# A spectral filter and an MLP in one kernel: the first batch's last inverse pair by way of DRAM, with four first-stage units of the second batch in front of it

## The chip, the cores and the metric

The kernel runs on one core of one Trainium2 chip. A core has TensorE (PE, matrix products), VectorE (DVE), ScalarE (ACT), GpSimd (POOL), and SyncE (SP), which here only issues DMAs; DMAs are also issued from ACT's and POOL's queues. The metric is the device time of one execution in microseconds (us).

## The reference

```
x: (8, 3008, 256)   filt: (1505, 256) complex   w_in: (256, 2048)   w_out: (2048, 256)   all float32
X = rfft(x, axis=1);  y = irfft(X * filt, n=3008, axis=1)          # for each of 8 batches
h = y.reshape(24064, 256) @ w_in
out = (h * clip(h + 3, 0, 6) / 6) @ w_out
```

## The kernel before

**The transform.** 3008 = 47 x 64, so the real FFT is done in two stages for 24 frequencies k of the stage of 47. Stage 1 (`a_unit`: 16 small matmuls over 4 of the 32 columns, eight units for a batch) writes an intermediate z to DRAM (`z_store`, four DMAs a unit). Stage 2 (`b_unit`) reads it back, `f_unit` multiplies by the filter on DVE, `y_unit` forms the complex products, and `bi_unit` is the first stage of the inverse; its result g goes to DRAM (`g_store`, two DMAs of 256 KB). The units of stage 2 go by two k each, 12 units (0 to 11) for a batch; `bi_unit` takes two units at once, and is called here *pair 0, 2, ... 10* by its first unit. The second stage of the inverse (`n_first`, `n_unit`, `n_five`) reads g back transposed into the tile `t4`, k on partitions, multiplies it with a table and leaves the tokens of y in the SBUF ring `xn`.

**The MLP.** The 24064 tokens are worked off in 47 blocks of 512, each in 8 steps of 256 hidden columns. Block 0 is done plainly: in step p `plain_up(p)` (L789) makes the hidden values, ACT the relu (L726), DVE the gate g (`hswish`, L731), and `plain_down(p-1)` (L800) multiplies the previous step's g by w_out. From block 1 on a Strassen-like scheme is used (L681, L757).

**The weights** come as 64-bit words (`load_bits`, 16 parts of 512 KB) and are turned into float32: ACT takes the absolute high word (`w_abs`, L321), DVE does seven operations (`w_conv`, `w_conv_2`, L330 to L353). `convert(n)` does n parts in one go, `convert_half` one half of a part; the list `(3, 3, 3, 4, 4, 3, 2, 2)` says how many halves follow the gates of each step of block 0.

**Order.** Nothing is rearranged: each engine's instructions stand in the order in which the program text issues them. Batch 0 is transformed ahead of block 0, all units in a row; from then on `places(n)` says at which step (counted over all blocks) a unit of batch n is done, and `at(step, ...)` plans it.

**Batch 0's own way.** Stage 1 of batch 0 (`a0_unit`) leaves z in SBUF, in the space of `xn` and `xs`, and `turn(c)` transposes it for stage 2, unit pairs c = 0 to 5. Block 0's tokens need all 12 units. Pairs 0 to 6 go through DRAM in full and come back by `first_load`. Pair 8 goes through DRAM with only the rows that block 0 needs (`g0_first`, four small stores, two from ACT, two from SP), its full store following later. Pair 10's units, and pair 8's again in part k = 20 to 23, don't wait for DRAM: `direct(NU - 2)` and `direct(NU - 1)` multiply the y of units 10 and 11 straight with a table `direct_t` (1.13 MB, loaded in two DMAs) into the same PSUM banks to which `n_first` then adds the products of the k that came through DRAM:

```
        for i in 1, 2:
            w_abs(i)
        direct(NU - 2)
        direct(NU - 1)
        bi_unit(0, NU - 2, ...)      # its store is for later blocks
        ...
        n_first()
```

**Buffers that matter.** `s1` (in pool `sp`) and `t1` have two buffers each, `t3` one, `t2` three; `xs` holds three parts of x. A DMA issued on SP also waits, by the program's semaphores, until the eighth DMA before it has landed.

Of the kernel before, what the change touches and what calls it, by code (L numbers as in the profile page):

```python
# [55 lines left out]
ATOM = 2 * KH  # L56
FIRST = tuple(range(NJ + 1, 0, -1))
# [19 lines left out]
def _make_tables():  # L77
# [76 lines left out]
    direct = np.zeros((P, TC, ND))  # L154
    for k in range(KH):
        for j in range(HC):
            for (ri, hh), x in terms(k, j, rows).items():
                if j in FIRST:
                    first[hh * 64 + ri * 32 + k, FIRST.index(j)] = first_of(x, FIRST.index(j))
                if j < 2:  # L160
                    ones[ri * ATOM + hh * KH + k, j] = cs_of(x)
            if j in FIRST:
                for (ri, hh), x in terms(k, j, late_rows).items():
                    last[ri * ATOM + hh * KH + k, FIRST.index(j)] = cs_of(x)
            if j > 1:
                c, s = (terms(k, j, rows)[0, hh][0] for hh in range(2))
                for hh, v in enumerate((c, s)):
                    groups[hh * KH + k, j] = groups[HALF + hh * KH + k, j] = v
        if k >= KH - TC:
            for q in range(64):  # L170
                fr = k + NA * q if q < 32 else NA * (q - 31) - k
                for n, j in enumerate(FIRST):
                    th = [2 * np.pi * ((fr * rows(j, h, a)) % N) / N for h in range(2)]
                    direct[q, k - KH + TC, n * TOK:(n + 1) * TOK] = 2 / N * first_of(np.cos(th), n)
                    direct[HALF + q, k - KH + TC, n * TOK:(n + 1) * TOK] = -2 / N * first_of(np.sin(th), n)
    wai = np.concatenate([t.reshape(P, -1) for t in (groups, ones, first, last)], axis=1)
    f = np.float32
    return wa.astype(f), wai.astype(f), wb.astype(f), wi.astype(f), wf.astype(f), start.astype(f), direct.astype(f)
# [3 lines left out]
def kernel(  # L182
# [11 lines left out]
    wa_np, wai_np, wb_np, wi_np, wf_np, start_np, direct_np = _make_tables()  # L194
# [6 lines left out]
    direct_d = nc.inline_tensor(direct_np, name="direct_t").ap()  # L201
# [104 lines left out]
    def w_load(i, q):  # L306
        if W_AT[i] == "g":
            t = gp.tile([P, 7, 256], FP32, name="g")
            st["rest"] = t[:, 4:7, :].rearrange("p a n -> p (a n)")
# [123 lines left out]
    def a_unit(b, c):  # L433
        xc = xs[:, (b * NB + c) % 3, :, :]
        t = t1p.tile([P, XC // 2, 2, D], FP32, name="t1")
        ps = [bank(b).rearrange("p (j d) -> p j d", d=D) for h in range(2)]
        for j in range(2):
            for g in range(2):
                for h in range(2):
                    nc.tensor.matmul(ps[h][ts(g, 64), j, :], wa[ds(h * 64, NA), ds((c * XC + 2 * g + j) * 2 * KH, 64)],  # L440
                                     xc[ds(h * 64, NA), 2 * g + j, :], start=True, stop=True)
        for h in range(2 if b == 1 and c < NB - 2 else 1):
            nc.scalar.activation(out=t[:, :, h, :], in_=ps[h], func=AXT.Copy)
        st["t1", b, c] = t, ps[1]
# [68 lines left out]
    def y_unit(b, i):  # L513
        s1, s2 = st["y", b, i]
        if b == 0 and i % 2 == 0:
            st["y0"] = t1p.tile([P, 2, 2, D], FP32, name="t1")
        y = yp.tile([P, 2, D], FP32, name="y") if b else st["y0"][:, i % 2, :, :]
# [6 lines left out]
    def bi_unit(b, i, ps=None):  # L524
        ys = [st.pop(("y", b, i + v)) for v in range(2)]
        ps = ps or [psF.tile([P, 2, D], FP32, name="psf", tag="f") for ri in range(2)]
        for v, ri in ((0, 0), (1, 0), (0, 1), (1, 1)):

            products = isinstance(ys[v], tuple)
            w, y = (wi[:, 1 + ri, :], ys[v][ri]) if products else (wi[ts(ri, 64), 0 if b else 3, :], ys[v][ts(ri, 64)])  # L530
# [6 lines left out]
    def g0_first(i):  # L537
        t = st["t3", 0, i]
        for v in range(2):
            for h in range(2):  # L540
                (nc.scalar, nc.sync)[v].dma_start(g_d[0, ds(h * HC + 1, NJ + 1), :, ds(2 * (i + v), 2), :].rearrange("c ri u d -> c ri (u d)"),
                                    t[ds(v * 64 + h * HC + 1, NJ + 1)].rearrange("p ri u d -> p ri (u d)"))
# [96 lines left out]
    def direct(i):  # L639
        if "psn" not in st:  # L640
            st["psn"] = {(c, dh): (psO.tile([P, 2, 2, P], FP32, name="po%d" % (2 + dh)).rearrange("p a u m -> p (a u m)")
                                   if c else psF.tile([P, 512], FP32, name="psn", tag="f"))
                         for c in range(2) for dh in range(2)}
        for u in range(2):
            k = 2 * i + u - KH + TC
            for (c, dh), ps in st["psn"].items():
                t, n = c * NJ * TOK, (1 if c else NJ) * TOK
                nc.tensor.matmul(ps[:, 0:n], st["y", 0, i][:, u, ts(dh, P)], st["direct"][k][:, ds(t, n)],
                                 start=k == 0, stop=False, skip_group_check=True)

    def n_first():
        for (c, dh), ps in st.pop("psn").items():
            for q, j in enumerate(chunks[c][1]):
                nc.tensor.matmul(ps[:, ts(q, TOK)], t4[:, j - 1, ts(dh, P)], edges[:, FIRST.index(j), :],
                                 start=False, stop=True, skip_group_check=True)
            to = xn[:, dh, :, 0:PAIRS]
            if c == 0:
                nc.scalar.activation(out=to[:, :, 0:NJ * NA].rearrange("p h (j a) -> p j h a", a=NA),
                                     in_=ps[:, 0:NJ * TOK].rearrange("p (j h a) -> p j h a", j=NJ, h=2), func=AXT.Copy)
                continue  # L660
            nc.scalar.activation(out=to[:, :, NJ * NA:], in_=ps[:, 0:2 * NX].rearrange("p (h a) -> p h a", h=2), func=AXT.Copy)
# [230 lines left out]
    with tc.manual_schedule():  # L892
# [93 lines left out]
        g_store(0, NU - 4)  # L986
        g_store(0, NU - 2)
        for c in range(2):
            x_load(1, c)
            load_bits(7 + c)  # L990
        w_abs(3)
        convert(3)

        def wai_load():
            nc.sync.dma_start(wa[:, 528:], wa_d[:, 528:])
# [17 lines left out]
        at(2, x_load, 1, 2)  # L1013

# [49 lines left out]
        for n in range(1, B):  # L1064
            a_at, f_at, y_at, bi_at = places(n)
            for c, s in enumerate(a_at):
                at(s, a_unit, n, c)
                at(s, a_sums, n, c)
                at(s, z_store, n, c, nc.sync if n == 1 else nc.gpsimd)
                if c >= 3:  # L1070
# [3 lines left out]
            for c in range(NT):  # L1074
                s = f_at[2 * (c - TB) + (n == 1)] + 1 if c >= TB else a_at[-1] + 1
                at(s, t2_load, n, c)
                s = f_at[2 * (c - FB) + 1] + 1 if c >= FB else a_at[-1 if n > 1 else 3] + 1
# [110 lines left out]
```

## Time and profile before

| | |
|---|---|
| median of 3 runs | 2660.89 us (2660.49 to 2661.43) |
| the profiled execution | 2661.05 us, span of its trace 2659.2 us |
| batch 0's stage 2 and inverse, to the first product of block 0 | 25.4 to 65.3 us |
| direct products on PE (L648) | 52.0 to 60.7 us |
| `n_first` on PE (L654) | 62.1 to 65.0 us |
| block 0, steps 0 to 7 | 65.3 to 129.3 us |
| DVE busy between 65 and 130 us, of each 5 us | 4.1 to 4.9 |

Times are counted from the start of the span. In the lines of the profile the columns are the start and the length in us, the engine, the line of the program, the operation with output <- input, how many instructions, and in brackets the idle time before and what ended it. PEld is the load of a matmul's fixed operand, beside PE.

### The profile page before, as it was taken

Reading aid. Unit: us, or ns where it says so; the run is one execution under the profiler, and the core shown is the slowest. Engines: PE = TensorE matmul, PEld = TensorE weight load, DVE = VectorE, ACT = ScalarE, POOL = GpSimd, SP = SyncE. Lnnn points to the kernel's source line nnn. Section 1 sums busy time; section 2 is a strip of 40 time slices with the busy share of each in tenths; the row PEclk is TensorE's granted clock in tenths of the full one; section 3 lists DMA queues with packets and bytes.
Section 4 is the critical chain, followed back from the end, with each engine's and each line's share of the span. In section 5 each row is a group of like instructions: output and inputs, shape, how many; then the busy total and the mean of one; then the engine's idle time right before and its main releaser. Section 6 shows DMA issues by size and latency. Waiting matters only on the chain.

```text
span 2659.2 us, 54237 instructions
## 1 busy us (share of the span) xinstructions
PE 2642.1 (99%) x21584; PEld 2317.6 (87%) x21584; DVE 2058.6 (77%) x3503; ACT 1306.3 (49%) x2672; POOL 495.1 (19%) x731
## 2 busy tenths in 40 slices
PE   8999999999999999999999999999999999999999
PEld 6588888888888888888888888888888888899998
DVE  7978867877688876888768887688877878767666
ACT  3454444445545545455444545445455454454554
POOL 2252122111221112211031110311113120111110
PEclk9999999999999999999999999999999999999999
DMA  9732233212331123411223113231122421110000
GB/s 244 215 99 70 63 103 98 64 36 72 87 109 56 36 77 82 109 56 36 84 76 109 56 38 85 72 109 56 45 78 72 109 59 47 45 43 21 21 20 24
DMA packets 134818, 198.24 MB, mean 75 GB/s; under 512 B 23146, under 2 KB 99016, under 8 KB 134374
## 3 DMA queue, kind: packets, MB, share of 16 engines
q1 hardware_dynamic: 117037, 150.12, 19.8%
q0 software_dynamic: 16960, 44.16, 6.3%
q8 instruction: 170, 2.79, 0.4%
q14 instruction: 82, 0.67, 0.1%
q10 hardware_dynamic: 569, 0.50, 0.1%
HBM read 122.43 MB, written 83.98 MB: 78 GB/s over the span
## 4 chain that ended last, share of the span: by engine, by line
PE 95%; DVE 3%; DMA 1%; issue 0%; ACT 0%; SPq 0%; POOL 0%; POOLq 0%; DVEq 0%; ACTq 0%
PE po L757 43%; PE al L681 24%; PE be L681 18%; PE psn L621 2%; PE psf L531 2%; PE psf L440 2%; PE psf L487 1%; DVE g L731 1%; DMA w_all<-in_x_dram 0%; PE po L496 0%; PE po L800 0%; PE psn L632 0%; PE psf L496 0%; PE po L407 0%; DVE y L332 0%
## 5 line engine op out<-in xcount | busy, mean ns | idle before, releaser
L757 PEld LDWEIGHTS po<-w_all,g 128*128 128x128 f32 x10276 | 1362.3, 191 | 153.1 <-issue 44.1
L757 PE MATMUL po<-w_all,g 128*128 128x128 f32 x10276 | 1402.2, 276 | 0.2
L726 ACT ACTIVATE r<-h,half_c 128x512 f32<-128x512 f32 x736 | 531.0, 721 | 355.5 <-DVE h L707 343.5
L731 DVE SCALAR_TENSOR_TENSOR g<-r,h 128x512 f32<-128x512 f32 x736 | 531.3, 722 | 212.6 <-ACT r L726 200.3
L681 PE MATMUL al<-xt,w_all 128*128 128x256 f32 x2208 | 659.7, 381 | 0.1
L681 PE MATMUL be<-xt,w_all 128*128 128x256 f32 x1472 | 437.8, 379 | 0.0
L707 DVE TENSOR_TENSOR h<-be,s 128x512 f32<-128x512 f32 x368 | 253.9, 690 | 158.5 <-PE be L681 151.2
L681 PEld LDWEIGHTS al<-xt,w_all 128*128 128x128 f32 x2208 | 335.4, 192 | 1.0 <-POOL w_all L361 0.5
L681 PEld LDWEIGHTS be<-xt,w_all 128*128 128x128 f32 x1472 | 279.7, 190 | 37.9
L721 ACT ACTIVATE h<-al 128x256 f32<-128x256 f32 x368 | 141.4, 384 | 321.5 <-PE al L681 321.4
L712 DVE TENSOR_TENSOR h<-al,s 128x256 f32<-128x256 f32 x368 | 155.9, 424 | 150.2 <-PE al L681 149.1
L739 DVE TENSOR_TENSOR g<-g 128x512 f32<-128x512 f32 x367 | 261.4, 712 | 12.6
L702 ACT ACTIVATE s<-al 128x256 f32<-128x256 f32 x368 | 141.4, 384 | 194.5 <-PE al L681 191.1
L547 POOL DMA_DIRECT2D g_tmp<-t x96 | 55.3, 592 | 937.7 <-ACT t L534 937.7
L693 ACT ACTIVATE s<-be 128x256 f32<-128x256 f32 x368 | 141.4, 384 | 176.3 <-PE be L681 176.3
L681 PE MATMUL al<-xn,w_all 128*128 128x256 f32 x736 | 222.4, 384 | 1.4 <-DVE h L712 1.4
L681 PE MATMUL be<-xn,w_all 128*128 128x256 f32 x736 | 218.9, 379 | 0.0
L677 POOL TENSOR_TENSOR xt<-xn 128x256 f32<-128x256 f32 x184 | 135.8, 756 | 434.4 <-ACT xn L603 434.4
L738 DVE TENSOR_TENSOR g<-g 128x256 f32<-128x256 f32 x367 | 172.5, 470 | 12.5
L692 ACT ACTIVATE s<-al 128x256 f32<-128x256 f32 x368 | 141.4, 384 | 68.2 <-PE al L681 68.2
L741 DVE TENSOR_TENSOR g<-g 128x256 f32<-128x256 f32 x367 | 159.8, 435 | 12.5
L461 POOL DMA_DIRECT2D z_tmp<-t x192 | 95.2, 504 | 365.0 <-DVE t L454 347.6
(149 smaller groups left out, 1845.8 us busy)
## 6 DMA issues: line engine op xcount, KB each, us to landing
g_tmp<-t POOLq DMA_DIRECT2D x96, 256.0 KB, 3.7
t<-g_tmp SPq DMA_DIRECT2D x184, 120.0 KB
t<-z_tmp SPq DMA_DIRECT2D x42, 512.0 KB
z_tmp<-t POOLq DMA_DIRECT2D x192, 96.0 KB, 2.5
xs<-in_x_dram SPq DMA_DIRECT2D x112, 128.0 KB
o_tmp<-o SPq DMA_DIRECT2D x46, 256.0 KB
ft<-in_filt_r_dram SPq DMA_DIRECT2D x168, 64.0 KB
ft<-in_filt_i_dram SPq DMA_DIRECT2D x168, 64.0 KB
```

The lines of the kernel that those rows point to most:

```text
L681: nc.tensor.matmul(ps, w_in[p][:, w, :], x, start=start, stop=stop, skip_group_check=True)
L692: nc.scalar.activation(out=s[:, 0, :], in_=al, func=AXT.Copy)
L693: nc.scalar.activation(out=s5, in_=be[:, 1, :], func=AXT.Copy)
L702: nc.scalar.activation(out=s[:, 1, :], in_=al, func=AXT.Copy)
L707: nc.vector.tensor_tensor(out=st["h"][0].rearrange("p (a n) -> p a n", a=2), in0=be, in1=s, op=ALU.add)
L712: nc.vector.tensor_tensor(out=st["h"][1][:, 256:512], in0=al, in1=s5, op=ALU.add)
L726: nc.scalar.activation(out=r, in_=st["h"][i], func=AXT.Relu, bias=half_c, scale=1.0 / 6.0)
L731: nc.vector.scalar_tensor_tensor(out=st["g", k, p][:, o:o + 2, :].rearrange("p a n -> p (a n)"), in0=st["r", i], scalar=1.0, in1=st["h"][i ...
L738: v.tensor_tensor(out=g[:, G1, :], in0=g[:, G3, :], in1=g[:, G22, :], op=ALU.add)
L739: v.tensor_tensor(out=g[:, G3:G2 + 1:2, :], in0=g[:, G3:G1 + 1, :], in1=g[:, G11:G11 + 1, :].broadcast_to([P, 2, 256]), op=ALU.subtract)
L741: v.tensor_tensor(out=g[:, G4, :], in0=g[:, G12, :], in1=g[:, G2, :], op=ALU.subtract)
L757: nc.tensor.matmul(st["po", k][bank][:, part, u, :], g[:, a, ts(u, P)], w_out[p][:, w, :], start=(p == 0 and n in OPENS and u == 0), stop= ...
```

## The change

The direct products and their table are taken out. Pair 10 goes through DRAM like the others; pairs 8 and 10 are stored in full from SP, and `first_load` fetches k = 20 to 23 after the others. Four stage-1 units of batch 1 (`EARLY_A = 4`) move from steps 2 to 5 of block 0 to a place around `bi_unit(0, 10)`, ahead of `n_first`; the first three use `t2` buffers for their results, and the PSUM banks of `po0` to `po3`. For these, `wa` is loaded whole in one DMA (0.8 MB) after pair 0, three parts of x after pair 6, and the `z_store`s of the four units are issued from POOL instead of SP. `w_abs(3)` joins 1 and 2 ahead of these units; `convert(2)` takes the place of `convert(3)`, and steps 0 and 1 of block 0 get four halves instead of three. The other four units of batch 1 stand at steps 0, 2, 3 and 5, and its stage 2 begins at step 9 instead of 12.

```diff
+EARLY_A = 4
...
     def a_unit(b, c):
         xc = xs[:, (b * NB + c) % 3, :, :]
-        t = t1p.tile([P, XC // 2, 2, D], FP32, name="t1")
-        ps = [bank(b).rearrange("p (j d) -> p j d", d=D) for h in range(2)]
+        if b == 1 and c < EARLY_A - 1:
+            t = t2p.tile([P, TC, D], FP32, name="t2").rearrange("p (j s) d -> p j s d", s=2)
+        else:
+            t = t1p.tile([P, XC // 2, 2, D], FP32, name="t1")
+        ps = [bank(b > 1 or c >= EARLY_A).rearrange("p (j d) -> p j d", d=D) for h in range(2)]
...
-    def g_store(b, i):
+    def g_store(b, i, q=nc.gpsimd):
         t = st.pop(("t3", b, i))
         for v in range(2):
-            nc.gpsimd.dma_start(g_d[b, :, :, ds(2 * (i + v), 2), :].rearrange("c ri u d -> c ri (u d)"),
+            q.dma_start(g_d[b, :, :, ds(2 * (i + v), 2), :].rearrange("c ri u d -> c ri (u d)"),
                                 t[ts(v, 64)].rearrange("p ri u d -> p ri (u d)"))
...
     def n_first():
-        for (c, dh), ps in st.pop("psn").items():
-            for q, j in enumerate(chunks[c][1]):
-                nc.tensor.matmul(ps[:, ts(q, TOK)], t4[:, j - 1, ts(dh, P)], edges[:, FIRST.index(j), :],
-                                 start=False, stop=True, skip_group_check=True)
...
+        one = bank(0).rearrange("p (e n) -> p e n", e=2)
+        for dh in range(2):
+            for c in range(2):
+                ps = one[:, dh, :] if c else psF.tile([P, 512], FP32, name="psn", tag="f")
+                for q, j in enumerate(chunks[c][1]):
+                    nc.tensor.matmul(ps[:, ts(q, TOK)], t4[:, j - 1, ts(dh, P)], edges[:, FIRST.index(j), :],
+                                     start=q == 0 and c * dh == 0, stop=True, skip_group_check=True)
...
-        last = x0_at(HC * D - 2048, 3 * ND)
-        nc.sync.dma_start(last, direct_d[:, 0:3, :].rearrange("p k n -> p (k n)"))
         load_bits(3)
-        st["direct"] = [last[:, ts(k, ND)] for k in range(3)] + [st["rest"][:, 0:ND]]
-        nc.sync.dma_start(st["direct"][3], direct_d[:, 3, :])
...
                 b_unit(0, i)
                 f_unit(0, i)
-                if c == NT - 1:
-                    y_unit(0, i)
             if c + 1 < NT:
                 turn(c + 1)
             if c:
                 bi_unit(0, 2 * c - 2)
-                (g0_first if c == NT - 1 else lambda i: g_store(0, i))(2 * c - 2)
+                g_store(0, 2 * c - 2, nc.gpsimd if c < NT - 1 else nc.sync)
+            if c == 1:
+                nc.sync.dma_start(wa, wa_d)
             if c == 4:
+                for j in range(3):
+                    x_load(1, j)
                 first_load(0, KH - 3 * TC)
+        for i in 1, 2, 3:
+            w_abs(i)
+        a_unit(1, 0)
+        x_load(1, 3)
         first_load(KH - 3 * TC, KH - TC)
-        for i in 1, 2:
-            w_abs(i)
-        direct(NU - 2)
-        direct(NU - 1)
-
-        bi_unit(0, NU - 2, [psU.tile([P, 512], FP32, name=n).rearrange("p (u d) -> p u d", u=2) for n in ("al", "be")])
+        bi_unit(0, NU - 2)
+        g_store(0, NU - 2, nc.sync)
+        for j in range(1, EARLY_A):
+            a_unit(1, j)
+        x_load(1, EARLY_A)
+        first_load(KH - TC, KH)
+        for j in range(EARLY_A):
+            z_store(1, j, nc.gpsimd)
         load_bits(6)
-        nc.sync.dma_start(wa[:, 0:528], wa_d[:, 0:528])
         nc.sync.dma_start(wf, wf_d)
         n_first()
-        g_store(0, NU - 4)
-        g_store(0, NU - 2)
-        for c in range(2):
-            x_load(1, c)
-            load_bits(7 + c)
-        w_abs(3)
-        convert(3)
+        x_load(1, EARLY_A + 1)
+        load_bits(8)
+        convert(2)
...
-        for s, n in enumerate((3, 3, 3, 4, 4, 3, 2, 2)):
+        for s, n in enumerate((4, 4, 3, 4, 4, 3, 2, 2)):
...
             if n == 1:
-                return (list(range(2, NB + 2)), [12, 13, 15, 18, 19, 20, 22, 23, 26, 27, 28, 30],
-                        [14, 15, 16, 19, 21, 22, 24, 25, 27, 29, 30, 31], [16, 21, 24, 29, 31, 32])
+                return (list(range(2 - EARLY_A, 2)) + [0, 2, 3, 5], [9, 12, 14, 18, 19, 20, 22, 23, 26, 27, 28, 30],
+                        [13, 15, 16, 19, 21, 22, 24, 25, 27, 29, 30, 31], [16, 21, 24, 29, 31, 32])
```

In `bi_unit` of the new program units 10 and 11 use the products of `f_unit` directly, as all other units of batch 0 do, with no `y_unit`.

More of the change, by code (lines that the diff above doesn't have):

```diff
@@ L153, in _make_tables @@
     last = np.zeros((P, NJ + 1, TOK))
-    direct = np.zeros((P, TC, ND))
     for k in range(KH):
@@ L168, in _make_tables @@
                     groups[hh * KH + k, j] = groups[HALF + hh * KH + k, j] = v
[L169 to L175, printed above, removed]
     wai = np.concatenate([t.reshape(P, -1) for t in (groups, ones, first, last)], axis=1)
     f = np.float32
-    return wa.astype(f), wai.astype(f), wb.astype(f), wi.astype(f), wf.astype(f), start.astype(f), direct.astype(f)
+    return wa.astype(f), wai.astype(f), wb.astype(f), wi.astype(f), wf.astype(f), start.astype(f)
 @with_exitstack
@@ L192 @@
     nc = tc.nc
-    wa_np, wai_np, wb_np, wi_np, wf_np, start_np, direct_np = _make_tables()
+    wa_np, wai_np, wb_np, wi_np, wf_np, start_np = _make_tables()
     wa_d = nc.inline_tensor(wa_np, name="wa_t").ap()
@@ L200 @@
     start_d = nc.inline_tensor(start_np, name="start_t").ap()
-    direct_d = nc.inline_tensor(direct_np, name="direct_t").ap()
     z_d = nc.dram_tensor("z_tmp", (B, KH, 2, HC, 2, D), FP32, kind="Internal").ap()
@@ L308, in w_load @@
             t = gp.tile([P, 7, 256], FP32, name="g")
-            st["rest"] = t[:, 4:7, :].rearrange("p a n -> p (a n)")
             t = t.bitcast(I32)[:, 0:4, :].rearrange("p a n -> p (a n)")
@@ L514, in y_unit @@
         s1, s2 = st["y", b, i]
-        if b == 0 and i % 2 == 0:
-            st["y0"] = t1p.tile([P, 2, 2, D], FP32, name="t1")
-        y = yp.tile([P, 2, D], FP32, name="y") if b else st["y0"][:, i % 2, :, :]
+        y = yp.tile([P, 2, D], FP32, name="y")
         re, im = slice(0, HALF), slice(HALF, P)
@@ L521, in y_unit, with bi_unit @@
         st["y", b, i] = y
-    def bi_unit(b, i, ps=None):
+    def bi_unit(b, i):
         ys = [st.pop(("y", b, i + v)) for v in range(2)]
-        ps = ps or [psF.tile([P, 2, D], FP32, name="psf", tag="f") for ri in range(2)]
+        ps = [psF.tile([P, 2, D], FP32, name="psf", tag="f") for ri in range(2)]
         for v, ri in ((0, 0), (1, 0), (0, 1), (1, 1)):
             products = isinstance(ys[v], tuple)
-            w, y = (wi[:, 1 + ri, :], ys[v][ri]) if products else (wi[ts(ri, 64), 0 if b else 3, :], ys[v][ts(ri, 64)])
+            w, y = (wi[:, 1 + ri, :], ys[v][ri]) if products else (wi[ts(ri, 64), 0, :], ys[v][ts(ri, 64)])
             nc.tensor.matmul(ps[ri][ts(v, 64)], w, y, start=True, stop=True)
@@ L535, in bi_unit @@
         st["t3", b, i] = t
[L537 to L542, printed above, removed]
-    def g_store(b, i):
+    def g_store(b, i, q=nc.gpsimd):
         t = st.pop(("t3", b, i))
         for v in range(2):
-            nc.gpsimd.dma_start(g_d[b, :, :, ds(2 * (i + v), 2), :].rearrange("c ri u d -> c ri (u d)"),
+            q.dma_start(g_d[b, :, :, ds(2 * (i + v), 2), :].rearrange("c ri u d -> c ri (u d)"),
                                 t[ts(v, 64)].rearrange("p ri u d -> p ri (u d)"))
@@ L636, in n_unit @@
             ready(i)
[L639 to L649, printed above, removed]
@@ L651, in n_first @@
-    def n_first():
-        for (c, dh), ps in st.pop("psn").items():
-            for q, j in enumerate(chunks[c][1]):
-                nc.tensor.matmul(ps[:, ts(q, TOK)], t4[:, j - 1, ts(dh, P)], edges[:, FIRST.index(j), :],
-                                 start=False, stop=True, skip_group_check=True)
[L656 to L661, printed above, removed]
+    def n_first():
+        one = bank(0).rearrange("p (e n) -> p e n", e=2)
[5 more added lines that the diff above has]
+                                     start=q == 0 and c * dh == 0, stop=True, skip_group_check=True)
+                to = xn[:, dh, :, 0:PAIRS]
+                if c == 0:
+                    nc.scalar.activation(out=to[:, :, 0:NJ * NA].rearrange("p h (j a) -> p j h a", a=NA),
+                                         in_=ps[:, 0:NJ * TOK].rearrange("p (j h a) -> p j h a", j=NJ, h=2), func=AXT.Copy)
+        for dh in range(2):
+            ps = one[:, dh, :]
+            nc.scalar.activation(out=xn[:, dh, :, ds(NJ * NA, NX)], in_=ps[:, 0:2 * NX].rearrange("p (h a) -> p h a", h=2),
+                                 func=AXT.Copy)
@@ L971 @@
                 bi_unit(0, 2 * c - 2)
-                (g0_first if c == NT - 1 else lambda i: g_store(0, i))(2 * c - 2)
+                g_store(0, 2 * c - 2, nc.gpsimd if c < NT - 1 else nc.sync)
+            if c == 1:
+                nc.sync.dma_start(wa, wa_d)
             if c == 4:
+                for j in range(3):
+                    x_load(1, j)
                 first_load(0, KH - 3 * TC)
+        for i in 1, 2, 3:
+            w_abs(i)
+        a_unit(1, 0)
+        x_load(1, 3)
         first_load(KH - 3 * TC, KH - TC)
-        for i in 1, 2:
-            w_abs(i)
-        direct(NU - 2)
-        direct(NU - 1)
-        bi_unit(0, NU - 2, [psU.tile([P, 512], FP32, name=n).rearrange("p (u d) -> p u d", u=2) for n in ("al", "be")])
+        bi_unit(0, NU - 2)
[6 more added lines that the diff above has]
+            z_store(1, j, nc.gpsimd)
         load_bits(6)
-        nc.sync.dma_start(wa[:, 0:528], wa_d[:, 0:528])
         nc.sync.dma_start(wf, wf_d)
         n_first()
-        g_store(0, NU - 4)
-        g_store(0, NU - 2)
-        for c in range(2):
-            x_load(1, c)
-            load_bits(7 + c)
-        w_abs(3)
-        convert(3)
+        x_load(1, EARLY_A + 1)
+        load_bits(8)
+        convert(2)
         def wai_load():
-            nc.sync.dma_start(wa[:, 528:], wa_d[:, 528:])
             nc.sync.dma_start(wai, wai_d[:, 0:NW])
         half = 0
-        for s, n in enumerate((3, 3, 3, 4, 4, 3, 2, 2)):
+        for s, n in enumerate((4, 4, 3, 4, 4, 3, 2, 2)):
             for i in range(n):
@@ L1012 @@
         at(0, wai_load)
-        at(2, x_load, 1, 2)
         n_at = {0: -2, 1: -2}
@@ L1066 @@
             for c, s in enumerate(a_at):
+                if n == 1 and c < EARLY_A:
+                    continue
                 at(s, a_unit, n, c)
@@ L1069 @@
                 at(s, z_store, n, c, nc.sync if n == 1 else nc.gpsimd)
-                if c >= 3:
+                if c >= (3 if n > 1 else EARLY_A + 2):
                     at(max(a_at[c - 3], s - 6), x_load, n, c)
@@ L1076 @@
                 at(s, t2_load, n, c)
-                s = f_at[2 * (c - FB) + 1] + 1 if c >= FB else a_at[-1 if n > 1 else 3] + 1
+                s = f_at[2 * (c - FB) + 1] + 1 if c >= FB else a_at[-1] + 1
                 at(s, table_load, n, c)
```

## The prediction

> **What bounds the kernel now.** I read the page's busy shares first, then the chain of waits between 40 and 135 us, then the timelines of TensorE (PE), VectorE (DVE), ScalarE (ACT) and SyncE's queue (SP) over the same stretch.
>
> ```profile
> PE 2642.1 (99%) x21584; PEld 2317.6 (87%) x21584; DVE 2058.6 (77%) x3503; ACT 1306.3 (49%) x2672; POOL 495.1 (19%) x731
> ```
>
> PE is busy for 99% of the span and gapless from about 130 us on, so what happens before 130 us moves the whole rest by its own size. The change lies there. The chain through it (start us, us, what):
>
> ```profile
> 49.14 1.92 PE psf L531 x8
> 51.08 0.61 ACT t L534
> 51.71 4.35 DMA g_tmp<-t
> 56.08 2.33 DMA g_tmp<-t
> 58.74 3.25 DMA t<-g_tmp
> 62.08 2.46 PE psn L654 x20
> 64.56 0.47 ACT xn L658
> 65.27 1.98 PE al L789 x4
> ```
>
> The round trip of pair 8 through DRAM (51.7 to 62.0, the store of six rows only, then the load) ends last, and PE's timeline shows what hides it: the direct products (L648).
>
> ```profile
> 52.03 1.81 PE L648 MATMUL psn<-w_all,t 128*128 128x470 f32 x4 [1.02 <-ACT t L534]
> ...
> 60.08 0.58 PE L648 MATMUL po<-g,t 128*128 128x94 f32 x4
> ...
> 62.08 2.44 PE L654 MATMUL psn<-wai,t 128*128 128x94 f32 x20 [0.40 <-DMA t<-g_tmp]
> ...
> 77.16 1.98 PE L789 MATMUL al<-xn,w_all 128*128 128x512 f32 x4 [0.84 <-DVE g L731]
> ```
>
> So PE waits only 1.02 + 0.40 us. The last line shows the second bound: in the eight steps of block 0 (65.27 to 129.3 us) PE waits for DVE's g, because DVE, busy 4.7 of every 5 us there, works off the weight conversions (4.2 us each) between the g's.
>
> Three prices, from the timeline of DVE, the page's DMA issues (KB each, median us to landing) and the timeline of PE:
>
> ```profile
> 59.12 0.69 DVE L353 SCALAR_TENSOR_TENSOR w_all<-s,y 128x512 f32<-128x512 f32 x1
> ```
> ```profile
> g_tmp<-t POOLq DMA_DIRECT2D x96, 256.0 KB, 3.7
> ```
> ```profile
> 2.78 3.78 PE L939 MATMUL al<-r 128*128 128x512 f32 x4 [2.78 <-ACT r L933]
> ```
>
> A conversion ends with L353 (this one began at 55.55 and took 4.26); a 256 KB store takes 3.7 us from issue to landing; and the kernel's first matmuls, after idleness, take 3.78 / 4 = 0.945 us each where the same shape takes 1.98 / 4 = 0.495 at 77.16.
>
> **What the Trainium skill says.** "DMA: Bandwidth & Descriptors", section "Anatomy of one DMA": about 2.0 us fixed plus the bytes at 436 GB/s, most of the 2 us being the receipt of the write. The trace agrees: the small store at 56.08 took 2.33. The same page, "Issuing engines are not separate DMA queues": transfers issued by SP and POOL share the same 16 engines; so POOL stores beside the critical ones cost them bandwidth. "TensorE: Matmul & The Clock Gate", Part 1: an idle window of about 3.4 us halves PE's clock, and about 3.4 us of work restores it. L939 agrees with the half clock; no later wait of PE in the trace of before is over 1.1 us, so a second fall is not shown there.
>
> **The change, step by step**, on the clock of before. Pairs are named by their first unit.
>
> *1. Removed.* 32 direct products (52.03 to 60.6: 8.5 us of PE), four y operations on DVE (4 x 0.72 = 2.9), two table loads (1.13 MB), four small stores. What was cover is gone together with what it covered; the last pair (10) now makes the same trip.
>
> *2. When pair 10 is ready.* DVE's two f_units start at 48.37 and, without y between them, end at 48.37 + 6 x 0.715 = 52.65. PE is done with pair 8 at 51.0 and with the first a_unit at 52.1, so bi_unit(10) runs from 52.65 to 54.5.
>
> *3. A new wait on ACT.* Before, w_abs(3) stood after n_first (65.38). Now three w_abs stand ahead of the copies of a_unit(1,0) and of bi_unit(10), and their tile s1 has two buffers. The third must wait until DVE's conversion 1 has read the first: 52.65 + 4.26 = 56.9. ACT takes its instructions in order, so behind w_abs(3) (0.65, to 57.55) come the a_unit's copies (1.09, to 58.6) and bi_unit(10)'s (1.08, to 59.7). Who waits: the store of pair 10, and a_units 2 and 3, whose banks these copies free.
>
> *4. SP's queue.* Ahead of the store stand three x_loads from 45.6 on (turn(5) must have read xs), 12 issues of 0.42 us, partly held because each DMA on SP also waits for the eighth before it to land (the 0.8 MB load of wa among them): done about 51.6. Then first_load(0,12), 4 issues to 53.5; pair 8's stores, now 2 x 256 KB, issued 53.7 to 54.6, landing about 57.7 (3.7 + the second issue); x_load(1,3) in between; then first_load(12,20), which waits for that landing: 57.8 to 59.4. So SP and ACT free the store of pair 10 at about the same time: 59.8.
>
> *5. The trip.* The second store is issued at 60.3 and lands 3.7 later: 64.0 (POOL's z_stores of 96 KB run beside it from 58.7 on; skill's price alone: 63.0). x_load(1,4)'s issues (1.8) fit in between. Then first_load(20,24): three more issues of 0.45 and the measured 3.25 of the last one: 68.6. **n_first starts at 69.0** instead of 62.08. The a_units end about 62, so PE idles about 7 us.
>
> *6. n_first* has the same 24 matmuls and six copies (3.2 us to the first matmul of block 0), with four small copies behind the last instead of beside: 3.4. Block 0 starts at 72.4 instead of 65.27: **+7.1**. After 7 us of idleness I take half clock for a part of n_first: 0 to 3 us, taken **+1.5**.
>
> *7. Block 0.* DVE now does two conversions, not three, before it, and would be idle from 61 to about 75; the half more in each of steps 0 and 1 (2 x 2.1 us) falls into a stage where DVE sets the pace. Recomputed step by step with up 3.6, down 3.56, a_unit 1.02, half 2.1, g 0.6: step 2 begins 14.1 after the start of block 0 (before 11.9), step 5 41.7 (before 38.8), step 8 67.4 (before 64.0): +3.4. Two a_units leave steps 8 and 9 (-2.05); two others leave steps where PE waited for DVE and save nothing. Net **+1.3** (-0.5 to +3). The moved z_stores leave SP; POOL has nothing else before about 100 us, so that is free; if POOL were late, only DRAM reads after step 6 would notice. The batch-1 steps moved from 12 and after to 9 and after lie in a stretch without PE gaps: 0.
>
> *Sum:* 7.1 + 1.5 + 1.3 = +9.9 on the profiled execution's 2661.05 us (span 2659.2); the median of the runs is 0.16 less, so **2670.8**.
>
> **Unknown costs, both ends.** Store to landing: 2.6 (skill) to 6 (pair 4's store, issued at 44, landed about 50 under load). SP before the store: 57.5 to 63. Half clock: 0 to 3. Block 0: -0.5 to +3. All favourable together give n_first at 66.5 and +4.2; all unfavourable +17.
>
> **Rivals.**
> A. *The cover is enough* (the other side): the trip is done when the a_units are, PE never waiting: bi_unit(8) to 51.0, four a_units 4.1, bi_unit(10) to 54.5, so n_first at 57.6 and block 0 at 60.9: -4.4 + 1.3 = -3.1, 2657.8. Against it: even from 54.5, two copies (1.1), 2.6 and 0.4 for the stores and 4.6 for the loads make 63.2. Not slower by 0.2% as long as n_first starts by 65.9 (even at 60.6); it needs the copies by 56 and SP free by then, and both queues speak against it.
> B. *Neither queue holds*, or only partly: w_abs(3) finds its buffer, the loads go faster, the store leaves at 57.5: n_first 66.7, half clock for less: 2667.
> C. *DMA contention:* x_loads (1.5 MB with x_load(1,3)), wa and POOL's stores stretch SP's waits so that the pair-10 store leaves at 62 to 63: n_first 72, half clock in full: 2676.
> D. That the round trip is off the path after all is excluded: xn, all of block 0's input, is made from it.
>
> **Numbers.** A measurement here can tell about 0.2%, 5.3 us, from no change. Chances: forecast 0.60, B 0.15, C 0.15, A 0.10. A and a good part of the lowest end of B lie within 0.2%: same 0.10, faster 0.02, slower 0.88. The range leaves out A's 0.10 and the top of C: 2665 to 2678.
>
> **What would show it.** Right: L541 and L648 gone; in the chain a store and a load of g_tmp with about 9 us from the ACT copies to n_first; n_first at 67 to 71; ACT's L321 waiting for DVE L353 ahead of those copies; PE idle some 7 us; first matmuls of n_first at twice their time; step 2 of block 0 some 14 us after its first. Wrong: n_first before 66, or PE without idleness there, or block 0 shorter than 65 us.

## The result, and the profile after

The changed kernel takes **2687.36 us** (median of 4 runs, 2685.97 to 2688.17) beside 2661.16 (4 runs, 2660.49 to 2661.47): ratio 1.0100, 95% interval 1.0087 to 1.0112. It is slower by 26 us, where 10 were forecast and 17 was given as the worst end of the bounds. The profiled execution took 2687.11 with a span of 2685.0 (before 2661.05 and 2659.2), so the 25.8 us by which its span is longer are nearly the whole difference, and the rest of this section looks for them there.

First the page: the busy shares and the granted clock in 40 slices of 67 us.

```profile
PE 2644.5 (98%) x21552; PEld 2318.6 (86%) x21552; DVE 2055.6 (77%) x3499; ACT 1310.6 (49%) x2673; POOL 502.0 (19%) x743
...
PEclk9799999999999999999999999999999999999999
```

PE has 2.4 us more busy time with 32 matmuls fewer, and slice 2 (67 to 134 us) has a clock of 0.7 to 0.8, where before has at least 0.9 throughout. So PE does the same work and loses its time around that slice. The timeline of PE (start, duration, line, [idle before it, and who ended it]):

```profile
58.73 1.88 PE L434 MATMUL po<-xs,wa 47*64 47x256 f32 x16 [2.52 <-ACT t L437]
61.39 2.58 PE L434 MATMUL po<-xs,wa 47*64 47x256 f32 x16 [0.78 <-DMA xs<-in_x_dram]
76.19 2.42 PE L630 MATMUL psn<-wai,t 128*128 128x94 f32 x10 [12.21 <-DMA t<-g_tmp]
...
81.91 3.78 PE L767 MATMUL al<-xn,w_all 128*128 128x512 f32 x4 [0.32 <-ACT xn L638]
85.49 2.73 PE L767 MATMUL be<-xn,w_all 128*128 128x512 f32 x4
...
98.67 1.98 PE L767 MATMUL al<-xn,w_all 128*128 128x512 f32 x4 [2.35 <-DVE g L709]
...
115.69 2.82 PE L434 MATMUL psf<-xs,wa 47*64 47x256 f32 x16 [3.78 <-DMA xs<-in_x_dram]
118.44 5.13 PE L778 MATMUL po<-w_all,g 128*128 128x256 f32 x16
...
156.71 0.59 PE L659 MATMUL al<-xt,w_all 128*128 128x256 f32 x2
```

Four marks cut it up: `n_first` (L630), the first `plain_up` of block 0 (L767, "up" from here on), the end of block 0 (the first L659), the end of the span. In before the end of block 0 is this line:

```profile
129.30 0.59 PE L681 MATMUL al<-xt,w_all 128*128 128x256 f32 x2
```

| mark | before, us | after, us | the stage up to it grew by |
|---|---|---|---|
| `n_first` starts | 62.08 | 76.19 | 14.1 |
| block 0 starts | 65.27 | 81.91 | 2.5 |
| block 0 ends | 129.30 | 156.71 | 10.8 |
| span ends | 2659.2 | 2685.0 | -1.6 (two `a_unit`s fewer from there on) |

So the cover of four `a_unit`s leaves PE idle for 12.21 us, not 7; and block 0 itself, 64.0 us before, now lasts 74.8. The first is best read from SP's timeline, since SP carries pair 10's store and the last `first_load`. The *trip*, in what follows, is the time from the first issue of that store to `n_first`.

```profile
57.03 2.11 SPq L371 DMA_DIRECT2D xs<-in_x_dram  x4
60.18 1.34 SPq L564 DMA_DIRECT2D t<-g_tmp  x4
61.63 1.51 SPq L532 DMA_DIRECT2D g_tmp<-t  x2
63.24 7.69 SPq L371 DMA_DIRECT2D xs<-in_x_dram  x4
71.05 1.34 SPq L564 DMA_DIRECT2D t<-g_tmp  x4
```

The store of pair 10 (L532) leaves at 61.63. Then the four issues of x_load(1,4), which fetches part 4 of batch 1's x, last 7.69 us, where the same four took 2.11 at 57.03. One of them is 3.33 us long, as the chain of waits shows, and it is the instruction itself: the chain has 0.04 us ahead of it, and the one wait that SP's waits give for these issues is 0.8 us (for PE, at the first of the four). Only at 71.05 comes the last `first_load` (L564), whose data the chain has landing at 76.05. POOL's timeline and the page of DMA issues for 59 to 73 us show what ran beside it:

```profile
59.46 4.96 POOL L455 DMA_DIRECT2D z_tmp<-t  x10 [8.49 <-ACT t L437]
```
```profile
z_tmp<-t POOLq DMA_DIRECT2D x16, 96.0 KB, 6.1
```

These are the moved z_stores of the four early units, 16 x 96 KB from 59.46 to 71.4, landing 6.1 us after issue, where the median of the whole execution is 2.5.

### The profile page after: what moved, and what is told of

Read it like the earlier page. It is cut to its first block, busy times and chain, and to the rows that moved or that the text cites. A ratio compares the mean times of both kernels' runs of the same rounds, so it can differ in the third digit from the quotient of the medians.

```text
span 2685.0 us, 54160 instructions
## 1 busy us (share of the span) xinstructions
PE 2644.5 (98%) x21552; PEld 2318.6 (86%) x21552; DVE 2055.6 (77%) x3499; ACT 1310.6 (49%) x2673; POOL 502.0 (19%) x743
## 4 chain that ended last, share of the span: by engine, by line
PE 94%; DVE 3%; DMA 1%; SPq 1%; issue 0%; ACT 0%; POOL 0%; POOLq 0%; DVEq 0%; ACTq 0%
PE po L735 43%; PE al L659 24%; PE be L659 17%; PE psn L606 2%; PE psf L434 2%; PE psf L523 2%; PE psf L481 1%; PE po L778 1%; DVE g L709 1%; DMA xs<-in_x_dram 1%; DMA w_all<-in_x_dram 1%; PE po L490 0%; SPq L371 0%; PE psf L490 0%; PE psn L617 0%
## 5 line engine op out<-in xcount | busy, mean ns | idle before, releaser
L659 PE MATMUL al<-xt,w_all 128*128 128x256 f32 x2208 | 659.5, 381 | 0.0
L659 PE MATMUL be<-xt,w_all 128*128 128x256 f32 x1472 | 437.9, 379 | 0.0
L659 PEld LDWEIGHTS al<-xt,w_all 128*128 128x128 f32 x2208 | 335.4, 192 | 0.4 <-issue 0.2
L659 PEld LDWEIGHTS be<-xt,w_all 128*128 128x128 f32 x1472 | 279.6, 190 | 38.3 <-ACT s L671 0.4
L532 POOL DMA_DIRECT2D g_tmp<-t x92 | 53.2, 592 | 924.7 <-ACT t L526 922.1
L659 PE MATMUL al<-xn,w_all 128*128 128x256 f32 x736 | 222.5, 384 | 2.3 <-DVE h L690 2.3
L659 PE MATMUL be<-xn,w_all 128*128 128x256 f32 x736 | 218.9, 379 | 0.0
L455 POOL DMA_DIRECT2D z_tmp<-t x208 | 103.2, 505 | 376.3 <-DVE t L448 348.5
```

Source lines behind the costliest of these rows:

```text
L659: nc.tensor.matmul(ps, w_in[p][:, w, :], x, start=start, stop=stop, skip_group_check=True)
```

## Experiments

Each kernel is the changed kernel ("after") with one edit, or several, unless said otherwise. The table comes first; times are medians with the 95% interval of the ratio to before; the marks are those of its profiled execution.

| kernel | us | ratio | `n_first` | block 0 starts | block 0 ends |
|---|---|---|---|---|---|
| after | 2687.36 | 1.0087 to 1.0112 | 76.19 | 81.91 | 156.71 |
| e1_z_late | 2681.81 | 1.0055 to 1.0089 | 72.31 | 78.04 | 152.42 |
| e2_x4_after | 2686.32 | 1.0074 to 1.0104 | 75.06 | 80.79 | 155.73 |
| e8_trip (e1 and e2) | 2680.90 | 1.0058 to 1.0088 | 71.36 | 77.09 | 150.58 |
| e5_abs_late | 2686.49 | 1.0080 to 1.0110 | 75.85 | 81.57 | 155.67 |
| e3_warm | 2685.38 | 1.0072 to 1.0102 | 77.02 | 80.36 | 153.68 |
| e6_conv3 | 2683.79 | 1.0067 to 1.0100 | 76.89 | 82.61 | 153.89 |
| e4_x6_early | 2685.50 | 1.0072 to 1.0102 | 77.09 | 82.82 | 155.90 |
| e7_x6_zpool | 2686.17 | 1.0078 to 1.0108 | 76.13 | 81.85 | 154.66 |
| b2_order | 2673.69 | 1.0030 to 1.0060 | 73.71 | 77.05 | 142.92 |
| b3_nowarm | 2675.64 | 1.0033 to 1.0066 | 71.56 | 77.29 | 144.98 |

### The trip: POOL's stores, or SP's order?

**e1_z_late** takes POOL's stores away from the trip, and issues the last unit's store on SP after `n_first`:

```
-        for j in range(EARLY_A):
-            z_store(1, j, nc.gpsimd)
...
         x_load(1, EARLY_A + 1)
+        z_store(1, EARLY_A - 1, nc.sync)
...
+        for j in range(EARLY_A - 1):
+            at(4, z_store, 1, j, nc.gpsimd)
```

> The z_stores of the four early units leave the stretch before n_first: three go to POOL after block 1's sums (step 4), the fourth to SP after n_first's loads. Theory 1 (POOL's z_stores share the DMA engines with SP's critical transfers and stretch x_load(1,4)'s four issues, which took 7.7 us): the four issues shrink to about 2 us, the loads of g start about 5 us earlier, n_first at 70 to 71 instead of 76.2, time 5 to 6 us shorter (about 2681.5). Rival (SP holds itself: each of its DMAs waits for the eighth before it, and these are slow for another reason): x_load(1,4) still takes over 6 us, n_first moves by less than 1.5 us, time within 1.5 us of the changed kernel's 2687.

SP's timeline of e1:

```profile
63.05 1.17 SPq L532 DMA_DIRECT2D g_tmp<-t  x2
64.33 2.51 SPq L371 DMA_DIRECT2D xs<-in_x_dram  x4
67.25 1.30 SPq L564 DMA_DIRECT2D t<-g_tmp  x4
```

The four issues are back at 2.51 us, and the last load leaves 3.8 us earlier although the store leaves 1.4 later. `n_first` starts at 72.31 (70 to 71 were expected) and the time falls by 5.5 us. The stores on POOL's queue did stretch SP's issues. The trip is 72.31 - 63.05 = **9.3 us**; the forecast's is 69.0 - 59.8 = 9.2, the changed kernel's 76.19 - 61.63 = 14.6.

**e2_x4_after** leaves POOL's stores where they are and changes only the order on SP:

```
-        x_load(1, EARLY_A)
         first_load(KH - TC, KH)
+        x_load(1, EARLY_A)
```

> x_load(1,4) stands behind the last first_load on SP instead of ahead of it. If the four issues of x_load(1,4) are what the loads of g waited for, these start when pair 10's stores have landed: with landing 3.7 us after the second issue (62.6), at about 66.5, n_first at 71 to 72, time 4 to 5 us shorter (about 2682.5). Rival (the stores themselves land only at about 70.9 because POOL's z_stores slow them): n_first stays at 75 to 76, no change within 1 us.

SP's timeline of e2:

```profile
61.80 1.16 SPq L532 DMA_DIRECT2D g_tmp<-t  x2
69.92 1.36 SPq L564 DMA_DIRECT2D t<-g_tmp  x4
```

Nothing stands between them, and still 7.0 us pass from the end of the stores' issue (62.96) to the load, which waits for them to land. The rival held: `n_first` starts only 1.1 us earlier, since the long x_load mostly filled a time in which the store was under way anyway. The trip is still 13.3 us. So the 7.69 us of issues are a sign, not the cause: pair 10's store itself is slow to land while POOL's stores run.

**e8_trip** puts both edits together.

> The first two edits together: POOL's stores of z for the early units moved behind the trip, and the last first_load ahead of the fourth x_load on SP. Theory (what made the trip longer than forecast is POOL's stores beside it, and the fourth x_load standing in SP's queue adds the rest): with POOL quiet the second store is issued at about 62.5, lands after 3 to 4 us at about 66, the loads take 4 us more, n_first at 70 to 70.5 (72.3 with the stores moved alone), the time 2679 to 2680. Rival (the last first_load waits for the landing of the stores anyway, so that the order on SP no longer matters once the issues are quick): n_first stays at 72 to 72.5 and the time at 2681 to 2682.5.

The chain of waits of e8, around the trip:

```profile
62.14 0.52 SPq L532
62.67 0.04 issue
62.71 3.58 DMA g_tmp<-t
66.33 0.04 issue
66.37 0.25 SPq L564
```

A store now lands in 3.58 us, and `n_first` starts at 71.36: between the two expectations, 1.0 us earlier than with e1 alone, and the time (2680.90) can't be told from e1's. The trip is 71.36 - 62.14 = **9.2 us**, as in e1; the 0.9 us by which `n_first` is earlier are there when the store leaves (62.14 for 63.05), ahead of the place where the two programs differ. So it is POOL's stores, and not the order on SP, that made 9.2 us into 14.6.

How they do it is less clear. Windows over the whole trip, of after, of e1 and of e8 (columns: window, its length, busy time of PE, PEld, DVE, ACT and POOL with their instructions, then PEclk, DMA share, GB/s):

```profile
61.60:76.20 14.60, 2.39 (x17) 1.12 (x16) 0.06 (x1) 1.59 (x4) 5.83 (x12) 0.50 0.74 214
```
```profile
63.00:72.30 9.30, 3.02 (x16) 1.11 (x17) 0.00 (x0) 1.08 (x2) 0.00 (x0) 0.50 0.72 194
```
```profile
62.10:71.40 9.30, 3.10 (x17) 1.22 (x17) 0.00 (x0) 1.09 (x2) 0.00 (x0) 0.50 0.59 132
```

The mean busy share of the 16 DMA engines doesn't tell a slow trip from a quick one: 0.74 in after, 0.72 in e1. What differs is how much is moved: 14.6 us at 214 GB/s make about 3.1 MB in after, against 1.8 MB in e1. But e1 also moves more than e8 (1.2 MB) and takes no longer. So the amount alone is not the rule either, and why POOL's stores in particular hold up SP's isn't shown.

**e5_abs_late** undoes the wait on ACT that the prediction found (step 3), by leaving w_abs(3) behind `n_first`:

```
-        for i in 1, 2, 3:
+        for i in 1, 2:
             w_abs(i)
...
         n_first()
+        w_abs(3)
```

> w_abs(3) goes back behind n_first, as in the kernel before; all else as in the changed kernel. It takes ACT's wait for DVE away: pair 10's copies end at about 56 instead of 60.15 and PE's 2.5 us wait in front of the third early unit goes. Theory (SP is as late as ACT: its middle first_load is issued at 60.2 to 61.5 for want of pair 8's stores): pair 10's stores still leave at about 61.5, n_first within 1.5 us of 76.2, time within 1.5 us of the changed kernel. Rival (ACT's wait sets the trip, as step 3 of the prediction has it alone): stores leave 3 us earlier or more, 3 us shorter.

The time is the same, as expected, but not for the expected reason: ACT's wait is gone, so the copies free z earlier, and POOL starts its stores at 55.30 instead of 59.46. SP's timeline of e5:

```profile
57.71 4.73 SPq L371 DMA_DIRECT2D xs<-in_x_dram  x4
62.92 3.31 SPq L564 DMA_DIRECT2D t<-g_tmp  x4
66.33 1.17 SPq L532 DMA_DIRECT2D g_tmp<-t  x2
```

Now x_load(1,3) and the middle `first_load`, 2.11 and 1.34 us in after, are the ones that swell, and pair 10's store leaves at 66.33. The swelling follows POOL's stores in time, whatever SP is issuing. And the trip itself, which begins when 12 of the 16 stores are issued, is back at 75.85 - 66.33 = 9.5 us. That is a second sign, from another side, that they are the cause.

### Block 0: the clock, the halves, the loads

**e3_warm** keeps PE at work through the wait, with 17 products of zeros that nothing reads:

```
+        warm = psU.tile([P, 512], FP32, name="al")
         for j in range(1, EARLY_A):
             a_unit(1, j)
+            for i in range((0, 3, 0, 14)[j]):
+                nc.tensor.matmul(warm, zero[:, P:2 * P], zero, start=True, stop=True)
```

> Adds 17 idle products of zeros on PE (3 after the second early unit, 14 after the fourth), in time in which PE waits. Theory (half clock after idleness): the granted clock stays at 1.00 up to n_first, n_first takes 3.2 us instead of 5.7 and the first products of block 0 3.7 instead of 6.3: 4.5 to 5 us shorter, about 2682.5; the second fall at 113 us (wait for x_load(1,6)) stays. Rival (the first block's start is set by DVE and ACT behind it, so a faster n_first is given back): less than 2 us shorter.

PE's timeline of e3:

```profile
63.20 13.98 PE L962 MATMUL al<-r 128*128 128x512 f32 x28
77.02 1.25 PE L630 MATMUL psn<-wai,t 128*128 128x94 f32 x10
...
80.36 1.98 PE L767 MATMUL al<-xn,w_all 128*128 128x512 f32 x4 [0.53 <-ACT xn L638]
...
94.51 3.59 PE L767 MATMUL al<-xn,w_all 128*128 128x512 f32 x4 [2.34 <-DVE g L709]
```

`n_first`'s ten products take 1.25 us instead of 2.42, the first up 1.98 instead of 3.78. The products ended late (77.02), which eats part: the clock fell once among them, from 63.65 to 67.06, and again just ahead of 94.51. Block 0 ends 3.0 us earlier; the median fell by 2.0, less than half of what was expected and just at the rival's bound, and the runs of the two kernels overlap (2684.20 to 2686.75 beside 2685.97 to 2688.17). So the trace shows what the half clock costs in these two places; that the whole kernel gains from the products is not clear of the noise.

**e6_conv3** gives DVE the third conversion back ahead of block 0, as before had it:

```
-        convert(2)
+        convert(3)
...
-        for s, n in enumerate((4, 4, 3, 4, 4, 3, 2, 2)):
+        for s, n in enumerate((3, 3, 3, 4, 4, 3, 2, 2)):
```

> convert(3) ahead of block 0 and halves (3, 3, 3, 4, 4, 3, 2, 2), as in the kernel before; all else as in the changed kernel. DVE, idle from 61.7 to 86.4 us, does the third conversion there. Theory (the two halves more in steps 0 and 1 are paid in full): up(2) starts 2.1 us and up(3) 3.4 to 4.2 us earlier after block 0's start; x_load(1,6) is on SP behind the same loads and is still waited for; 3 to 4 us shorter. Rival (the wait for x_load(1,6) in step 3 takes it all back, since SP's order is tied to the same conversions only in part): under 1.5 us shorter.

Block 0 lasts 71.3 us (153.89 - 82.61) instead of 74.8: 3.5 us, and the waits for g in front of steps 2 and 3 (2.35 and 1.17 us in after) are gone:

```profile
96.97 1.98 PE L767 MATMUL al<-xn,w_all 128*128 128x512 f32 x4
...
112.36 2.79 PE L434 MATMUL psf<-xs,wa 47*64 47x256 f32 x16 [3.58 <-DMA z_tmp<-t]
```

DVE's idle time ahead of block 0 (24.8 us in after) had room for it. The second line shows what stays: step 3's `a_unit(1,6)` still waits and then runs at half clock. (The line names a z_store, which landed last; the chain has the load of x, issued at 106.16, landing only 0.5 us before it.)

**e4_x6_early** and **e7_x6_zpool** take up that wait. In after, x_load(1,6) is issued at 109.76:

```profile
109.76 1.81 SPq L371 DMA_DIRECT2D xs<-in_x_dram  x4
```

It stands on SP in step 1 of block 0, behind a weight load, which waited 18 us for DVE to free its buffer, eight loads of `t4`, a z_store, x_load(1,7) and two more weight loads; its data land at 115.6. e4 issues it before block 0; e7 moves the z_stores of batch 1 to POOL as well:

```
         load_bits(8)
+        x_load(1, EARLY_A + 2)
...
-                at(s, z_store, n, c, nc.sync if n == 1 else nc.gpsimd)
+                at(s, z_store, n, c, nc.gpsimd)
-                if c >= (3 if n > 1 else EARLY_A + 2):
+                if c >= (3 if n > 1 else EARLY_A + 3):
```

(The two lines with z_store are e7's alone.)

> x_load(1,6) is issued behind x_load(1,5), before block 0, instead of in step 1, where it stands on SP behind a load of weight words that waits for a conversion on DVE. Theory: PE's 3.8 us wait for xs in step 3 and the half clock after it (a_unit 2.8 instead of 1.1, down product 5.1 instead of 3.7) go: up to 7 us at step 4, of which DVE, the next bound, gives back 2 to 3: 4 to 5 us shorter, about 2682.5. Rival (DVE's conversions set the pace anyway): under 1.5 us shorter.

> As the run in which x_load(1,6) is issued before block 0, and the z_stores of units 4 to 7 of batch 1 are issued from POOL instead of SP. There PE waited 4.6 us in step 4 for a copy into t1, whose z_store stood on SP behind words and loads of g. Theory: neither wait is left, nor the half clock after it; step 8 begins 68 to 70 us after block 0's start instead of 74.8, time 4.5 to 6 us shorter than the changed kernel. Rival (DVE's conversions are what is waited for in the end): step 8 at 73 us or later, under 2 us shorter.

PE's timeline of e7, step 4:

```profile
119.87 0.31 PE L606 MATMUL psn<-wai,t 48*64 48x47 f32 x2
124.76 2.38 PE L606 MATMUL psn<-wai,t 48*64 48x47 f32 x78 [4.58 <-DVE t L445]
```

The wait for x is gone in both, and 4.58 us of another stand in its place. It is for a copy on DVE (L445) of that same `a_unit`, which stands behind step 3's four conversion halves in DVE's queue and holds a PSUM bank that `n_five` needs. Block 0 lasts 73.1 and 72.8 us, 1.7 and 2.0 less; neither time can be told from after's, and of e7's two expectations the rival's is the nearer. So x was late, but DVE was next.

### All together

**b2_order** takes all these edits at once (e1, e2, e5, e6, e7, seven zero products), and puts pair 10's store ahead of x_load(1,3) and of the middle `first_load` on SP. **b3_nowarm** is the same without the zero products.

> All together: pair 10's stores ahead of x_load(1,3) and the middle first_load on SP, x_load(1,4) behind the last first_load, z_stores of the early units late, z_stores of units 4 to 7 on POOL, x_load(1,6) early, w_abs(3) late, three conversions ahead, and 7 products of zeros to keep PE busy. If the terms add: pair 10's stores leave at 57, land at 61, n_first at 66 to 68 without half clock, block 0 at 70 and step 8 at 134 to 135 (before: 129.3, with two units more to come): 2663 to 2666, so still 2 to 5 us over the kernel before, because the trip itself remains. Rival (transfers still collide, the three x parts with pair 8's and pair 10's stores): n_first after 71, 2670 or more.

> The combined version without the zero products: stores of pair 10 ahead of the fourth x_load, the x_load(1,6) early, z stores late, w_abs(3) after n_first, three conversions before block 0 and 3, 3, 3 halves. Theory (the zero products ran at half clock, ended at 73.7 and held n_first back without keeping the clock): n_first starts at 71 to 72 instead of 73.7, but first up(0) is at half clock in part, so the time is 2672 to 2675, as with them. Rival (the products kept what clock there was): n_first earlier, but block 0 starts at 79 or later and the time is 2677 or more.

b2 takes 2673.69 us, 13.7 less than after, and is still slower than before, ratio 1.0045 (1.0030 to 1.0060): its rival held. Its block 0 lasts 65.9 us against 64.0, so what remains lies nearly all ahead of block 0: `n_first` at 73.71 against 62.08. Part of that is the zero products, of which the last four took 5.37 us, most of it at half clock, and ended only at 73.9. b3's `n_first` is at 71.56, as expected, but then the half clock gives it back; the two can't be told apart by their times. No version tried brings `n_first` below 71.36 (e8), and none beats before. Why b3's `n_first` starts 6.2 us after its last `first_load` was issued (65.4), and not 4 as elsewhere, stays open.

## Why the prediction was wrong

The direction and most places were right; the size was not. By its own steps:

- *1 and 2, removed, and when pair 10 is ready.* Right: L541 and L648 are gone, and `bi_unit(10)` ran at 53.26, within 0.7 us of the forecast 52.65.
- *3, the new wait on ACT.* Right in place and size: ACT's timeline has the third L312 waiting 4.14 us for DVE's L344, and pair 10's copies end at 60.15 (forecast 59.7). In after SP came to the store only at 61.5, 1.4 us after the copies, so ACT was not the later one. e5 is no faster without the wait; but as POOL's stores came forward with it, e5 doesn't price the wait alone.

```profile
57.52 0.68 ACT L312 ACTIVATE s<-g 128x512 f32<-128x512 f32 x1 [4.14 <-DVE w_all L344]
```

- *4, SP's queue.* 1.8 us short: the store left at 61.63, not 59.8; the middle `first_load` began at 60.18, not 57.8, since pair 8's stores were issued 1.6 us later (55.26 for 53.7), and that load waits for them to land.
- *5, the trip.* **The step that failed.** It took 3.7 us for the store "(POOL's z_stores of 96 KB run beside it ...)" and let x_load(1,4)'s 1.8 us "fit in between". The trip took 14.6 us instead of 9.2. That 5.4 us and the 1.8 of step 4 are the 7.2 by which `n_first` was later than forecast. e1 shows 9.3 us once POOL's stores are out of the way, with the order on SP as the prediction had it. The prediction had named the Trainium skill's sentence that transfers issued by different engines share the 16 DMA engines ("DMA: Bandwidth & Descriptors", "Issuing engines are not separate DMA queues"), but put no number on it. The bound that it used, up to 6 us for a store under load, was close to the 7.0 seen in e2; but it stood in the list of unknown costs, and the estimate kept the unloaded value. (The low bound, 2.6 us, was not reached even in e8, with 3.58.) Step 7 even called POOL's stores free: they were looked at for who waits for them, not for whom they slow. Rival C had the mechanism, with the wrong transfers late: it let the store leave at 62 to 63 and land as usual.
- *6, `n_first` and the clock.* Mis-sized: "0 to 3 us, taken +1.5". It was 2.3 us in `n_first` (5.72 to the first up, forecast 3.4 at full clock) and 2.6 in the first up (81.91 to 88.15, 6.2 instead of 3.6), 4.9 in all. e3 bears most of it out: from `n_first` to the end of block 0 it takes 76.7 us (153.68 - 77.02) where after takes 80.5, 3.9 less. The upper end of the bound was too low, because the half clock lasted from about 60 to 87 us, and so through all of `n_first` and most of the first up; the prediction let it end within `n_first`.
- *7, block 0.* The halves were right: +3.4 forecast, 3.5 by e6. The two `a_unit`s less: -2.05 forecast, -1.6 seen. What was missing is the rest of the 10.8 us: besides the 2.6 of the clock, 10.8 - 2.6 - 3.5 = 4.7 us. The prediction looked at DVE's and PE's queues in block 0 and not at SP's, on which x_load(1,6) now stood behind weights and `t4` loads; that made a wait of 3.78 us and a second stretch of half clock, `plain_down` (L778) 5.13 us instead of 3.7. By the timelines step 3 alone is 7.1 us longer (108.21 to 123.40; before 85.37 to 93.48), and step 4, which has an `a_unit` less, 2.2 shorter. e4 and e7 show that not more than about 2 us of this could have been had by issuing it earlier, since DVE's copy is late next.

In sum, against the forecast +9.9: 7.2 from the trip and its queue, 3.4 from the clock (4.9 instead of 1.5), 4.7 from the rest of block 0, 0.1 from the halves and 0.5 from the two `a_unit`s; together 15.9, which is 25.8 - 9.9. The 4.7 is what is left over in this sum; that it is the wait in step 3 and the clock after it is read from the trace, and e4 and e7 remove only 2 of it.

The prediction's two ends don't come out of its own bounds: with all of them unfavourable (SP +3.2, landing +2.3, clock +1.5, block 0 +1.7 on the +9.9) the sum is +18.6, not +17, and with all favourable about +3.2, not +4.2. The result lies outside either way.

## What to carry to other kernels

When a latency-bound trip through DRAM becomes the path, count every transfer that runs beside it, on any queue: here 1.5 MB of stores that nobody waited for made a trip of 9.2 us into one of 14.6. Cover that is too short can cost twice: here PE idled for 12.2 us and then worked at half clock for 11 more; and when a change delays one stage, look at each queue of the next stage too, DMA queues included, for what is now due in another order. A wait taken away is worth only the distance to the next late thing: 4.58 us of DVE took the place of 3.78 us of a load.

## What the runs showed of the hardware

- A DMA issue on SP can itself be long. Under POOL's stores the four of x_load(1,4) took 7.69 us (elsewhere four in 2.1), one of them 3.33 with only 0.04 us ahead of it in the chain. What SP waits for inside the instruction isn't shown.
- The clock changes only on a grid of 3.41 us. The Trainium skill ("TensorE: Matmul & The Clock Gate", Part 1) tells of an activity window of 3413 ns that is free-running, not reset when the kernel starts, and gives one idle window for the fall and one of sustained work for the return. The traces agree on the grid; for the fall less idleness was enough here, and the return could take longer. These windows hold the changes, the first four rows from after, the next two from e3:

```profile
59.50:60.00 0.50, 0.50 (x14) 0.28 (x6) 0.50 (x1) 0.50 (x2) 0.50 (x2) 0.88 0.86 279
87.00:87.50 0.50, 0.50 (x2) 0.19 (x1) 0.14 (x1) 0.00 (x0) 0.00 (x0) 0.81 0.00 0
114.00:115.00 1.00, 0.00 (x0) 0.00 (x0) 0.96 (x4) 0.00 (x0) 0.00 (x0) 0.75 0.98 199
121.00:122.00 1.00, 1.00 (x5) 0.83 (x5) 0.90 (x2) 0.00 (x0) 0.00 (x0) 0.84 0.00 0
```
```profile
94.00:94.50 0.50, 0.00 (x0) 0.00 (x0) 0.50 (x2) 0.50 (x1) 0.00 (x0) 0.87 0.82 221
97.00:98.00 1.00, 1.00 (x3) 0.40 (x2) 0.96 (x2) 0.00 (x0) 0.00 (x0) 0.61 0.87 301
```

A mean of 0.88 over half a microsecond, made of 1.00 and then 0.50, puts the fall at 59.88. In the same way after returns at 87.19, falls again at 114.50 and returns at 121.32: stretches of 27.3, 27.3 and 6.8 us, which are 8, 8 and 2 times 3.41. e3 falls at 94.37 and returns at 97.78, once 3.41.

So it matters where on the grid a wait falls. Of e3's wait of 2.34 us (92.17 to 94.51) 2.20 lie in one window of its grid (90.96 to 94.37), and the clock fell at the end of it. The wait of 2.35 in after (96.32 to 98.67) is cut in two by an end at 97.43, and the clock stayed up. A wait well under 3.41 us was enough.

The return took 11 us of work in after, counted from `n_first` at 76.19. A whole window of the grid in `n_first` (first row) didn't bring it, the first whole window of up's products (second row) did:

```profile
77.00:80.30 3.30, 3.30 (x17) 3.30 (x17) 0.00 (x0) 0.57 (x1) 0.00 (x0) 0.50 1.03 280
83.80:87.10 3.30, 3.30 (x5) 1.33 (x4) 0.65 (x1) 0.69 (x1) 0.00 (x0) 0.50 0.01 2
```

PE counts as busy in both. e8 shows the same: no return in `n_first`, and one at 80.4, a window after up began at 77.09. That the kind of work (`n_first`'s small products with a weight load each) is the reason is likely from this, but no run tried it by itself.
